# Row sums on the evicting engine, paired copies, freed buffers and a written order: induced attention with a folded leaky FFN on one core

## The chip, the cores and the metric

The kernel runs on one core of a Trainium2 chip. The engines are TensorE (PE; its weight loads are shown apart as PEld), VectorE (DVE), ScalarE (ACT), GpSimd (POOL) and SyncE (SP), whose queue issues nearly all DMAs. The metric is the device time of an execution in microseconds, from the start of the program to its end, lower is better. The profile's span runs from the first to the last instruction of the profiled execution.

## The reference

```python
def mab(q, kv):
    s = scale * (q @ kv.transpose(0, 2, 1))
    s = s - s.max(-1, keepdims=True)
    a = np.exp(s)
    a /= a.sum(-1, keepdims=True) + 1e-09
    return a @ kv
h = mab(I, x)                    # I: inducing (32 x 128), the same for all 4 batches
y = mab(x, h).astype(np.float32) # x: 4 x 12480 x 128
...
h = y.reshape(49920, 128) @ w_in           # w_in: 128 x 2048
return np.maximum(0.01 * h, h) @ w_out     # w_out: 2048 x 128
```

The 32 inducing rows attend to all rows of a batch, which gives 32 rows `h`; every row of x then attends to those 32 rows, and its result passes a leaky feed-forward layer. Inputs x and inducing are float32; the two weights are float64 in memory.

## The kernel before

Each row that enters the feed-forward layer is a weighted mean of the 32 rows `h` of its batch. Where every hidden column has one clear sign over those rows, the leaky layer is linear in them, so `fixed_sign_path` folds w_in, the slopes and w_out into one 32 x 128 matrix for each batch (with a column of ones behind it, 129 wide), and the output is the second attention's weights times that matrix, divided by their sum. A flag says at the end whether all signs were clear; if not, a branch runs `any_sign_path` over everything. With these inputs the branch skips it.

A batch of 12480 rows is cut into six groups of 2048 rows (g = 0 to 5) and a small one of 192 (g = 6). The work is a set of named operations, each with a batch and a group (or step) number, here with their lines:

- First pass, for each group: `LD` loads x (L1797); `T` transposes four blocks on TensorE (L1848) and `C` copies each to SBUF, on ScalarE or VectorE (L1860); `S1` multiplies with the inducing rows (L1868); `E` copies the scores and takes their maximum (L1887). For steps of two or three groups `RD`, `X`, `NM`, `AL` make the running maximum, `W` the exponentials (L1933), `Y` a 32 x 32 transpose (L1942), `V` the sum of rows (L1964), `ZT` the sums of weights and `GA` the running h.
- Middle, for each batch: `ZP`, `RZ`, `HS`, `HP`, `HC` normalise h and copy it transposed (`hT`, L2000); `H`, `HT`, `SH`, `AH`, `G`, `FO`, `FC`, `SP`, `SC` make the hidden row (L2005), the signs, the slopes (`G` on POOL, L2030), the folded matrix and its copy (`folded`, L2052).
- Second pass, for each group: `S2` the scores against h (L1868), `LO` and `LE` their lowest value, `U` the exponentials into `uT` (L2081). `O` is the product with the folded matrix (L2099), four for a big group: halves h = 0, 1 and parts t = 0, 1, each two PSUM banks. `D` evicts it. On VectorE it adds 1e-9 to the four row sums in PSUM, takes the reciprocals and scales into `osb` (L2121 to 2123). On ScalarE it copies everything, sums included, to `stage` (L2117); then POOL adds 1e-9 (`DS`, L2135), VectorE takes the reciprocal (`DI`, L2140) and POOL scales (`DM`, L2145). `ST` stores the group (L2156).
- The weights come in eight pieces: `LW` loads 0.5 MB (L1802, L1804) into a buffer of `osb`, and `CA`, `CB`, `CO`, `CT`, `CP` turn float64 words into float32: a shift on POOL or ScalarE (L1812), a mask (L1816) and a join (L1822) on VectorE, a tail on ScalarE (L1828) and a sum on POOL (L1837).

The order comes from a planner (`Plan.ordered`): a list scheduler with estimated lengths, a rank and a lean for each operation, which also picks the engine of `C`, `D` and `CA`. All engines run their own instructions in that order; waits are semaphores. The buffers are counted in `BUFS` (xr 6, e 4, ay 4, uT 3, osb 3, stage 3), the PSUM banks of `O` in `banks_of` (two pairs, a third for the last batch).

## Time and profile before

| | us |
|---|---|
| median of 3 runs (lowest to highest) | 213.36 (212.34 to 214.01) |
| profiled execution | 212.81 |
| its span, first to last instruction | 211.0 |
| TensorE busy, share of the span | 183.1, 87% |
| VectorE | 155.9, 74% |
| ScalarE | 119.3, 57% |
| POOL | 109.0, 52% |
| mean granted TensorE clock | 0.949 |
| HBM read, written | 29.77 MB, 25.56 MB |

Busy time is the union of an engine's instructions. [...]

### The profile page before, as it was taken

To read this page: it belongs to the slowest core of one execution; us is meant where nothing else is said; L and a number is where in the kernel's file an instruction comes from. 1 tells how busy PE (TensorE), PEld (TensorE's weight loads), DVE (VectorE), ACT (ScalarE), POOL (GpSimd) and SP (SyncE) were. 2 spreads that over 40 slices of the span, in tenths; PEclk is the share of its full clock that TensorE was granted. 3 is DMA by queue.
4 is the path that set the end of the run, shared out by engine and by line. 5 is a ranking of instruction groups with operands and counts; after the bars stand their busy time and mean duration, and the time that the engine had idled before them with its cause. 6 is when DMAs were issued, how large, how long until landed. Compare 5 with 4: busy or idle time off the path is not lost.

```text
span 211.0 us, 6947 instructions
## 1 busy us (share of the span) xinstructions
PE 183.1 (87%) x2791; PEld 121.5 (58%) x2791; DVE 155.9 (74%) x519; ACT 119.3 (57%) x252; POOL 109.0 (52%) x162
## 2 busy tenths in 40 slices
...
GB/s 208 418 420 392 270 393 354 366 398 18 188 213 130 380 353 143 218 408 245 241 405 269 281 381 363 393 57 221 161 238 168 76 163 202 221 202 381 297 261 95
DMA packets 18794, 55.87 MB, mean 265 GB/s; under 512 B 1056, under 2 KB 2240, under 8 KB 15808
## 3 DMA queue, kind: packets, MB, share of 16 engines
...
q14 instruction: 18, 0.15, 0.2%
...
HBM read 29.77 MB, written 25.56 MB: 262 GB/s over the span
## 4 chain that ended last, share of the span: by engine, by line
PE 65%; DVE 12%; ACT 6%; DMA 5%; POOL 4%; issue 2%; SPq 0%; ACTq 0%; DVEq 0%; POOLq 0%
PE s_ps L1868 18%; PE xT_ps L1848 17%; PE po L2099 15%; PE h_ps L1964 8%; DMA raw<-in_moe_w_out_dram 5%; ACT xT L1860 3%; POOL osb L2145 3%; DVE osb L2123 2%; PE busy_ps L1767 2%; PE m_ps L2038 2%; ACT stage L2117 2%; DVE cv_a L1822 2%; PE H_ps L2005 1%; DVE ay L1942 1%; POOL cv_a L1812 1%
## 5 line engine op out<-in xcount | busy, mean ns | idle before, releaser
L2145 POOL TENSOR_TENSOR osb<-stage,inv 128x512 f32<-128x512 f32 (+1 forms) x67 | 67.0, 1010 | 20.1 <-DVE inv L2140 12.9
L2117 ACT COPY stage<-po 128x516 f32<-128x516 f32 (+1 forms) x67 | 37.0, 576 | 35.3 <-PE po L2099 33.5
L1848 PE MATMUL xT_ps<-ident,xr 128*128 128x128 f32 x384 | 52.0, 280 | 1.7 <-ACT xT L1860 0.8
L2099 PE MATMUL po<-folded,uT 32*128 32x129 f32 (+1 forms) x792 | 47.9, 309 | 4.2 <-ACT stage L2117 1.6
L1848 PEld LDWEIGHTS xT_ps<-ident,xr 128*128 128x128 f32 x384 | 41.3, 141 | 17.1 <-issue 3.9
L1860 ACT COPY xT<-xT_ps 128x512 f32<-128x512 f32 x74 | 40.2, 591 | 18.1 <-PE xT_ps L1848 15.9
L2099 PEld LDWEIGHTS po<-folded,uT 32*128 32x128 f32 (+1 forms) x792 | 37.3, 194 | 21.0 <-issue 9.4
L2135 POOL TENSOR_SCALAR inv<-stage 128x4 f32<-128x4 f32 (+1 forms) x67 | 14.9, 222 | 44.4 <-ACT stage L2117 41.3
L1868 PE MATMUL s_ps<-xT,indT 128*32 128x512 f32 x192 | 26.3, 617 | 1.4 <-ACT xT L1860 1.4
L1868 PE MATMUL s_ps<-xT,hT 128*32 128x512 f32 x192 | 24.8, 599 | 2.1 <-ACT uT L2081 2.0
L1964 PE MATMUL h_ps<-xr,ay 128*32 128x128 f32 x768 | 24.0, 274 | 2.5 <-DVE zg L1931 1.3
L2123 DVE TENSOR_TENSOR osb<-po,inv 128x512 f32<-128x512 f32 (+2 forms) x37 | 24.1, 651 | 1.3
L1887 DVE TENSOR_SCALAR_CACHE_REDUCE e<-s_ps 128x512 f32<-128x512 f32 (+1 forms) x28 | 17.1, 615 | 10.2 <-PE s_ps L1868 8.4
L1964 PEld LDWEIGHTS h_ps<-xr,ay 128*32 128x32 f32 x768 | 20.6, 110 | 6.3 <-issue 1.7
L2081 ACT ACTIVATE uT<-s_ps,least 128x512 f32<-128x512 f32 (+1 forms) x28 | 17.9, 640 | 10.2 <-DVE least L2071 9.9
L1812 POOL TENSOR_SCALAR cv_a<-raw 128x512 f32<-128x512 f32 x7 | 11.5, 1653 | 19.5 <-DMA raw<-in_moe_w_in_dram 16.1
L1933 ACT ACTIVATE e<-e,nm 128x512 f32<-128x512 f32 (+1 forms) x28 | 18.6, 669 | 2.7 <-DVE zg L1931 2.4
L1860 DVE COPY xT<-xT_ps 128x512 f32<-128x512 f32 x22 | 14.7, 679 | 6.5 <-ACT xT L1860 3.6
L1942 DVE STREAM_TRANSPOSE ay<-e 128x512 f32<-128x512 f32 (+1 forms) x28 | 17.3, 630 | 0.8 <-ACT e L1933 0.5
L2062 DVE TENSOR_REDUCE low<-s_ps 128x1 f32<-128x512 f32 (+1 forms) x28 | 17.0, 608 | 1.0 <-PE s_ps L1868 0.9
L2140 DVE RECIPROCAL inv<-inv 128x4 f32<-128x4 f32 (+1 forms) x67 | 10.6, 165 | 4.3 <-POOL inv L2135 3.4
L2121 DVE TENSOR_SCALAR inv<-po 128x4 f32<-128x4 f32 (+2 forms) x37 | 5.6, 151 | 5.7 <-PE po L2099 5.5
...
## 6 DMA issues: line engine op xcount, KB each, us to landing
out_dram<-osb SPq DMA_DIRECT2D x24, 1024.0 KB, 5.8
xr<-in_x_dram SPq DMA_DIRECT2D x23, 1024.0 KB, 7.8
raw<-in_moe_w_in_dram SPq DMA_DIRECT2D x4, 512.0 KB, 14.2
raw<-in_moe_w_out_dram SPq DMA_DIRECT2D x4, 512.0 KB, 8.5
xr<-in_x_dram SPq DMA_DIRECT2D x2, 512.0 KB, 4.5
...
```

Of the source, the lines that this page charges most:

```text
L1848: nc.tensor.transpose(pt[:, k * rows : (k + 1) * rows], xr[b, g][:rows, 4 * q + k, :], ident[:rows, :rows])
L1860: copying(engine)(xT[b, g][:, 4 * q : 4 * q + n, :].rearrange("p k t -> p (k t)"), V.pop(("T", b, g, q))[:, : n * rows],)
L1868: nc.tensor.matmul(ps[32 * j : 32 * j + 32, :w].rearrange("p (k r) -> p k r", r=32), lhsT, xT[b, g][:, :, 32 * j : 32 * j + 32], start=Tru ...
L1887: nc.vector.tensor_scalar(out=e[:rows], in0=V.pop(("S", b, g))[:rows, :w], scalar1=1.0, scalar2=None, op0=ALU.mult, op1=ALU.max, accum_out ...
L1933: nc.scalar.activation(e[:rows, :w], e[:rows, :w], AF.Exp, bias=nms[b, p][:rows], scale=SCALE, accum_out=zg[:rows])
L1942: nc.vector.transpose(t[:rows].rearrange("p k m -> p (k m)"), e[:rows, :w])
L1964: nc.tensor.matmul(hp[32 * (k % 4) : 32 * (k % 4) + 32, :], t[:rows, k, :], rows_in[:rows, k, :], start=(i == 0 and k < 4), stop=(last[k % ...
L2081: nc.scalar.activation(dst, src, AF.Exp, bias=least[:rows, b, g : g + 1])
L2099: nc.tensor.matmul(po[:m, j % 2, (P + 1) * i : (P + 1) * (i + 1)], uT[b, g][part, columns], folded[b % 2][part, :], start=True, stop=True, ...
L2117: nc.scalar.copy(raw[:m, :nj, : (P + 1) * n], src)
L2123: nc.vector.tensor_tensor(out=dst, in0=src[:, :, :, :P], in1=inv.unsqueeze(3).broadcast_to([m, nj, n, C]), op=ALU.mult)
L2145: nc.gpsimd.tensor_tensor(out=dst, in0=raw[:, :, :, :P], in1=inv.unsqueeze(3).broadcast_to([m, nj, n, C]), op=ALU.mult)
```

## The change

- The row sums of an `O` part are read from PSUM by the engine that evicts the part (`SA`: ScalarE or VectorE, +1e-9 into a small tile `inv` shared by both parts of a half). One reciprocal on VectorE (`RC`) serves both parts. `D` on ScalarE copies the 512 values alone; `D` on VectorE scales from PSUM after `RC`; POOL's `DM` needs `D` and `RC`. `DS` and `DI` are gone.
- The two copies `C` of a transposition pair that shares a PSUM tile run on one engine, both after the second transpose.
- The weight shift `CA` runs on ScalarE alone; `G` may run on VectorE, but the order keeps it on POOL.
- In the last batch `uT` is taken from the buffers of `e` and `ay` in turn, and `osb` of odd groups from those of `xr`; the last two big groups are stored in two halves.
- The order is written out; a letter behind a name picks the engine (a ScalarE, v VectorE, p POOL). `Plan.ordered` reads it and asserts that dependencies and buffers allow it. The planner, its ranks and leans are gone.
- Each engine gets a branch hint for the final branch, behind a marked instruction of the last batch, and the flag is read outside the hand-ordered block.

```diff
-    RANKS = {
...
+    ORDER = """
...
+        O0.4.0.0 D0.4.0.0a SA0.4.0.0a O0.4.0.1 SA0.4.0.1a D0.4.0.1a X1.2 NM1.2 AL1.2 W1.4 RC0.4.0 DM0.4.0.0
...
-    def cv_shift(i, engine):
+    def cv_shift(i):
...
-        multiply = nc.scalar.mul if engine == "ACT" else nc.gpsimd.tensor_scalar_mul
-        multiply(a.bitcast(F32), raws[i][:, :, 1].bitcast(F32), 2.0**-112)
+        nc.scalar.mul(a.bitcast(F32), raws[i][:, :, 1].bitcast(F32), 2.0**-112)
...
+    def weights_in(b, g):
+        return "uTr" if g == RG else "uT" if b < B - 1 else ("e", "ay")[g % 2]
+
+    def results_in(b, g):
+        return "xr" if b == B - 1 and g % 2 and g != RG else "osb"
...
+    def part_sums(b, g, h, t, engine):
+        n, m, nj, _ = results(b, g, h, t)
+        dst = V["inv", b, g, h][:m, 2 * t : 2 * t + nj, :n]
+        src = V["po", b, g, h, t][:m, :nj, P : (P + 1) * n : P + 1]
+        if engine == "ACT":
+            nc.scalar.activation(dst, src, AF.Copy, bias=1e-9)
+        else:
+            nc.vector.tensor_scalar_add(dst, src, 1e-9)
+
+    def part_inverse(b, g, h):
+        n, m, nj, _ = results(b, g, h, 1)
+        inv = V["inv", b, g, h][:m, : 2 + nj, :n]
+        nc.vector.reciprocal(inv, inv)
...
         if engine == "ACT":
-            V["raw", b, g, h, t] = raw = sb.tile([P, 2, 2 * P + 2], F32, tag="stage", name="stage", bufs=BUFS["stage"])
-            nc.scalar.copy(raw[:m, :nj, : (P + 1) * n], src)
-            return
...
-        inv = sb.tile([P, 2, 2], F32, tag="inv", name="inv", bufs=4)[:m, :nj, :n]
-        nc.vector.tensor_scalar_add(inv, src[:, :, :, P], 1e-9)
-        nc.vector.reciprocal(inv, inv)
...
+            V["raw", b, g, h, t] = raw = sb.tile([P, 2, 2, P], F32, tag="stage", name="stage", bufs=BUFS["stage"])
+            nc.scalar.copy(raw[:m, :nj, :n], src)
+        else:
+            nc.vector.tensor_tensor(out=dst, in0=src, in1=inverse_of(b, g, h, t)[4], op=ALU.mult)
...
-    def stage_sums(b, g, h, t):
...
-        nc.gpsimd.tensor_scalar_add(inv[:m, :nj, :n], raw[:, :, :, P], 1e-9)
-
-    def stage_inverse(b, g, h, t):
...
-    def store(b, g):
+        n, m, nj, dst, inv = inverse_of(b, g, h, t)
+        raw = V.pop(("raw", b, g, h, t))[:m, :nj, :n]
+        V["latest", "Pool"] = nc.gpsimd.tensor_tensor(out=dst, in0=raw, in1=inv, op=ALU.mult)
+
+    def store(b, g, j0, j1):
...
+                after=[("T", b, g, q | 1 if bank[0] != "tp" else q)], rank=at,
+                like=("C", b, g, q - 1) if q % 2 and bank[0] != "tp" else None,
...
+        for engine, mark in marks.items():
+            with tc.issue_after(mark):
+                tc.mark_branch_hint_location("general", hint="LikelyTaken", engines=[engine])
+        undecided = nc.values_load(flag[:1, :1], min_val=0, max_val=1)
+        with tc.If(undecided != 0, label="general"):
             any_sign_path(tc, x, inducing, w_in, w_out, out)
```

The table of the order, in instructions. SP's queue at the start of the program, before (`xr` is a group of x, `xrr` the small one, `raw` a piece of the weights):

```order
L1797 DMA xr<-in_x_dram 128x1024 x2
L1797 DMA xr<-in_x_dram 128x2048 x4
L1802 DMA raw<-in_moe_w_in_dram 128x1024 x3
L1797 DMA xr<-in_x_dram 128x2048
L1802 DMA raw<-in_moe_w_in_dram 128x1024
L1797 DMA xrr<-in_x_dram 96x256
L1797 DMA xr<-in_x_dram 128x2048 x2
L1804 DMA raw<-in_moe_w_out_dram 128x1024 x3
L1797 DMA xr<-in_x_dram 128x2048 x2
L1804 DMA raw<-in_moe_w_out_dram 128x1024
```

SP's queue at the same place now:

```order
L1652 DMA xr<-in_x_dram 128x1024 x2
L1652 DMA xr<-in_x_dram 128x2048 x3
L1657 DMA raw<-in_moe_w_in_dram 128x1024
L1652 DMA xr<-in_x_dram 128x2048 x2
L1652 DMA xrr<-in_x_dram 96x256
L1657 DMA raw<-in_moe_w_in_dram 128x1024 x2
L1652 DMA xr<-in_x_dram 128x2048 x2
L1657 DMA raw<-in_moe_w_in_dram 128x1024
L1659 DMA raw<-in_moe_w_out_dram 128x1024
L1652 DMA xr<-in_x_dram 128x2048
L1659 DMA raw<-in_moe_w_out_dram 128x1024 x3
```

Batch 0's last groups stand behind one piece of the weights instead of three and four, and the last three pieces behind one more group of batch 1. VectorE's queue up to batch 0's normalised h (`hc`), before (`cv_b` and `cv_a` are mask and join of a piece of the weights, `zn` the sum of weights, `e` the scores of a group of batch 1):

```order
L1816 TENSOR_SCALAR cv_b<-raw 128x512
L1822 SCALAR_TENSOR_TENSOR cv_a<-cv_a,cv_b 128x512
L1947 TENSOR_REDUCE z<-zg 128x1
L1950 TENSOR_SCALAR zn<-zn,al,z 128x1
L1887 TENSOR_SCALAR e,rm<-s_ps 128x512
L1987 TENSOR_SCALAR rz<-z_ps 128x1
L1988 RECIPROCAL rz<-rz 128x1
L1976 SCALAR_TENSOR_TENSOR hacc<-hacc,al,h_ps 128x128
L1992 TENSOR_SCALAR hc<-hacc,rz 128x128
```

VectorE's queue at the same place now:

```order
L1799 TENSOR_REDUCE z<-zg 128x1
L1802 TENSOR_SCALAR zn<-zn,al,z 128x1
L1670 TENSOR_SCALAR cv_b<-raw 128x512
L1676 SCALAR_TENSOR_TENSOR cv_a<-cv_a,cv_b 128x512
L1828 SCALAR_TENSOR_TENSOR hacc<-hacc,al,h_ps 128x128
L1743 TENSOR_SCALAR e,rm<-s_ps 128x512
L1828 SCALAR_TENSOR_TENSOR hacc<-hacc,al,h_ps 128x128
L1839 TENSOR_SCALAR rz<-z_ps 128x1
L1840 RECIPROCAL rz<-rz 128x1
L1670 TENSOR_SCALAR cv_b<-raw 128x512
L1844 TENSOR_SCALAR hc<-hacc,rz 128x128
```

The mask and join of piece 6 no longer stand ahead of the last sum; those of piece 4 stand behind it, and the mask of piece 5 between the reciprocal and `hc`. VectorE's queue at the first evictions of batch 3, before (`low` and `least` are the lowest scores, `osb` the output; the numbered `inv` belong to parts that ScalarE has copied):

```order
L2121 TENSOR_SCALAR inv<-po 128x4
L2122 RECIPROCAL inv<-inv 128x4
L2123 TENSOR_TENSOR osb<-po,inv 128x2x256
L2140 RECIPROCAL inv_3167<-inv_3167 128x4
L2070 STREAM_TRANSPOSE lows<-low 128x32
L2071 TENSOR_REDUCE least<-lows 128x1
L2062 TENSOR_REDUCE low<-s_ps 128x1
L2140 RECIPROCAL inv_3178<-inv_3178 128x4
```

VectorE's queue at the same place now:

```order
L1980 TENSOR_SCALAR inv<-po 128x4
L1985 RECIPROCAL inv<-inv 128x8
L1999 TENSOR_TENSOR osb<-po,inv 128x2x256
L1922 STREAM_TRANSPOSE lows<-low 128x32
L1923 TENSOR_REDUCE least<-lows 128x1
L1980 TENSOR_SCALAR inv<-po 128x4
L1985 RECIPROCAL inv<-inv 128x8
L1999 TENSOR_TENSOR osb<-po,inv 128x2x256
```

One reciprocal of eight stands where two of four stood, and it is ahead of the scaling of its own half.

## Rows read from the trace of the kernel before

**Rows 1.** Stretch, length, busy PE PEld DVE ACT POOL (instructions), clock, DMA share, GB/s.

```profile
5.30:24.40 19.10, 16.37 (x185) 11.07 (x184) 9.34 (x22) 11.34 (x23) 4.97 (x4) 1.00 0.96 387
24.40:45.60 21.20, 16.15 (x253) 10.96 (x254) 17.45 (x45) 12.60 (x29) 15.61 (x11) 0.93 0.98 368
45.60:165.00 119.40, 116.78 (x1889) 78.24 (x1893) 96.72 (x322) 77.71 (x169) 59.62 (x96) 1.00 0.67 249
...
178.30:203.00 24.70, 18.17 (x238) 12.90 (x230) 19.25 (x80) 10.15 (x19) 17.61 (x29) 0.79 0.68 261
203.00:211.00 8.00, 0.00 (x0) 0.00 (x0) 0.00 (x0) 0.00 (x0) 0.00 (x0) 0.50 0.45 157
```

**Rows 2.** Timeline, weight joins and hT of batch 0: start, us, engine, [idle before].

```profile
20.41 0.69 DVE L1822 SCALAR_TENSOR_TENSOR cv_a<-cv_a,cv_b 128x512 int32<-128x512 int32 x1
...
40.80 1.56 DVE L1822 SCALAR_TENSOR_TENSOR cv_a<-cv_a,cv_b 128x512 int32<-128x512 int32 x1
...
42.89 0.29 PE L1725 MATMUL z_ps<-zn,e 128*32 128x1 f32 x8 [2.29 <-DVE zn L1950]
...
45.62 0.21 ACT L2000 COPY hT<-hT_ps 128x64 f32<-128x64 f32 x1 [3.75 <-PE hT_ps L1725]
```

**Rows 3.** The page's groups: count, busy us, mean ns, idle us before.

```profile
L2135 POOL TENSOR_SCALAR inv<-stage 128x4 f32<-128x4 f32 (+1 forms) x67 | 14.9, 222 | 44.4 <-ACT stage L2117 41.3
L1812 POOL TENSOR_SCALAR cv_a<-raw 128x512 f32<-128x512 f32 x7 | 11.5, 1653 | 19.5 <-DMA raw<-in_moe_w_in_dram 16.1
L2140 DVE RECIPROCAL inv<-inv 128x4 f32<-128x4 f32 (+1 forms) x67 | 10.6, 165 | 4.3 <-POOL inv L2135 3.4
```

**Rows 4.** Groups with shapes kept apart, the same columns.

```profile
L2145 POOL TENSOR_TENSOR osb<-stage,inv 128x512 f32<-128x512 f32 x63 | 64.8, 1040 | 17.6 <-DVE inv L2140 12.9 <-DVE inv L2121 2.6 <-DVE rd L1896 0.7
L2117 ACT COPY stage<-po 128x516 f32<-128x516 f32 x63 | 35.7, 591 | 34.2 <-PE po L2099 32.5 <-POOL inv L2135 0.7
L2123 DVE TENSOR_TENSOR osb<-po,inv 128x512 f32<-128x512 f32 x33 | 22.8, 691 | 1.1
L1822 DVE SCALAR_TENSOR_TENSOR cv_a<-cv_a,cv_b 128x512 int32<-128x512 int32 x8 | 7.7, 963 | 1.5 <-POOL cv_a L1812 1.1
L2121 DVE TENSOR_SCALAR inv<-po 128x4 f32<-128x4 f32 x33 | 5.0, 153 | 5.7 <-PE po L2099 5.5
L1922 ACT ACTIVATE al<-nm 128x1 f32<-128x1 f32 x8 | 2.4, 296 | 5.4 <-DVE lower L1915 5.4
L2000 ACT COPY hT<-hT_ps 128x64 f32<-128x64 f32 x4 | 0.9, 220 | 3.7 <-PE hT_ps L1725 3.7
L1812 ACT ACTIVATE cv_a<-raw 128x512 f32<-128x512 f32 x1 | 0.7, 677 | 0.0
```

**Rows 5.** Chain that ended last: start, us, what; transposes in runs of eight and four.

```profile
59.20 1.02 PE xT_ps L1848 x8
...
62.91 0.59 PE xT_ps L1848 x4
```

**Rows 6.** Timeline of the last batch: start, us, engine, [idle before].

```profile
178.06 0.27 ACT L2052 COPY folded<-M_ps 128x128 f32<-128x128 f32 x1
...
183.14 1.06 PE L1868 MATMUL s_ps<-xT,hT 128*32 128x512 f32 x8 [1.33 <-ACT uT L2081]
...
192.81 3.23 PE L2099 MATMUL po<-folded,uT 32*128 32x129 f32 x32
...
202.19 1.25 SPq L2156 DMA_DIRECT2D out_dram<-osb  x2
```

**Rows 7.** DMA issues: count, KB each, median us from issue to landing.

```profile
out_dram<-osb SPq DMA_DIRECT2D x24, 1024.0 KB, 5.8
...
xr<-in_x_dram SPq DMA_DIRECT2D x2, 512.0 KB, 4.5
```

**Rows 8.** Instructions of the final branch: min/median/max ns, first and last start.

```profile
L2358 SPq EVENT_SEMAPHORE  x8: 17/17/17, 208.3 to 209.6; - x8
...
L2358 SPq COMPARE_BRANCH  x1: 45/45/45, 204.4 to 204.4; - x1
```

More of the change, by code (lines that the diff above doesn't have):

```diff
@@ new lines, in read @@
+    def read(self):
+        kinds = sorted({name[0] for name in self.ops}, key=len, reverse=True)
+        picks = {"a": "ACT", "v": "DVE", "p": "POOL"}
+        for word in self.ORDER.split():
+            kind = next(k for k in kinds if re.fullmatch(k + r"(\d+(\.\d+)*)?[avp]?", word))
+            at = word[len(kind) :].rstrip("avp")
+            name = (kind, *(int(i) for i in at.split(".") if i))
+            yield name, picks[word[-1]] if word[-1] in picks else next(iter(self.ops[name][0]))
@@ new lines, in ordered, with is_done @@
+    def ordered(self):
+        by, taken, order = {}, {}, []
+        def is_done(name):
+            only = self.ops[name][6]
+            while only is not None and only[0] in by and by[only[0]] != only[1]:
+                name, only = only[0], self.ops[only[0]][6]
+            return name in by
+        for name, engine in self.read():
+            lengths, emit, after, _, _, takes, _, extra, _, _, needs, like = self.ops[name]
+            assert engine in lengths and all(is_done(a) for a in after)
+            assert by.get(like, engine) == engine
+            assert engine not in needs or needs[engine] in by
+            for buffer in takes + extra.get(engine, []):
+                earlier = taken.setdefault(buffer[0], [])
+                n = len(earlier) - self.rooms[buffer[0]]
+                assert n < 0 or all(is_done(u) for u in self.users[earlier[n]])
+                earlier.append(buffer)
+            by[name] = engine
+            order.append((name, lambda emit=emit, engine=engine: emit(engine)))
+        assert all(is_done(name) for name in self.ops)
+        return order
@@ L2300, in second_pass @@
                 po, f = (banks_of(*part), *part), 1.0 if big else 0.4
-                first = [("osb", *key)] if h + t == 0 else []
+                first = [(otag, "O", *key)] if h + t == 0 else []
                 before = before_part
                 before_part = [("O", *part)]
-                add(("O", *part), {"PE": 0.446 * f}, lambda _, a=part: output(*a), mode="R",
-                    after=[("U", *key), ("SC", b)] + before, rank=at + 0.2, takes=[po] + first, uses=[po, (utag, *key), ("folded", b)], joins=("O", *key, h, 0) if t else None)
@@ L2311, in second_pass @@
-                add(("DI", *part), {"DVE": 0.18}, lambda _, a=part: stage_inverse(*a), after=[("DS", *part)], **staged_op)
-                add(("DM", *part), {"POOL": 1.05 * f}, lambda _, a=part: stage_scaled(*a), after=[("DI", *part)], **staged_op)
-                last += [("D", *part), ("DM", *part)]
-        add(("ST", *key), {"DMA": 2.55 if big else 1.2}, lambda _: store(b, g), rank=at - BEFORE,
-            after=last, uses=[("osb", *key)])
+                add(("O", *part), {"PE": 0.5 * f}, lambda _, a=part: output(*a), mode="R",
+                    after=[("U", *key), ("SC", b)] + before, rank=at + 0.2, takes=[po] + first + ([] if t else [("inv", *key, h)]), uses=[po, (utag, "U", *key), ("folded", b)], joins=("O", *key, h, 0) if t else None)
@@ new lines, in second_pass @@
+                add(("DM", *part), {"POOL": 1.02 if big else 0.55}, lambda _, a=part: stage_scaled(*a),
+                    after=[("D", *part), ("RC", *key, h)], only=(("D", *part), "ACT"), rank=at - 1,
+                    uses=[(otag, "O", *key), ("stage", *part), ("inv", *key, h)])
+                last += [("D", *part), ("DM", *part)]
+            add(("RC", *key, h), {"DVE": 0.17}, lambda _, h=h: part_inverse(*key, h), rank=at - 1,
+                after=[("SA", *key, h, t) for t in range(2)], uses=[("inv", *key, h)])
```

389 lines of the change are left out of this document (150 added, 239 removed), and 90 rows, old and new, of tables (LEANS, RANKS).

## Prediction

> **What bounds the kernel now.** I read the table of stretches first, then the timeline around the two places where it shows TensorE idle, then the groups for prices, and last the end of the program.
>
> The table [rows 1] splits the span at batch 0's small copy of h (45.6 us), at the end of the first passes (165), at the copy of batch 3's folded matrix (178.3) and at the last output work (203). From 45.6 to 165 TensorE is busy 116.78 of 119.40 us: that stage is bound by TensorE, and work taken off VectorE, ScalarE or GpSimd there is worth nothing. Outside it there is room. Up to 45.6 us TensorE is idle 2.73 + 5.05 us, and the granted clock of the second stretch is 0.93, so some 1.5 us more (0.07 of 21.2) are lost to the lower of its two levels: about 9 us. From 178.3 to 203 no engine is full (PE 18.17 of 24.70 at clock 0.79, DVE 19.25, POOL 17.61): the bound is the round trip from one engine to the next. The last 8.0 us hold no work.
>
> The timeline [rows 2] names the early gap. VectorE's weight joins (L1822) stand ahead of batch 0's last sum; one is 0.69 us at 20.41, another 1.56 us at 40.80. TensorE waits 2.29 us behind `zn`, and hT is copied only at 45.62. This wait, and not the DMA share of 0.98, ends last, although the joins themselves need weights that have landed.
>
> **The change, part by part.**
>
> *Row sums and GpSimd.* Removed: 67 additions on POOL at 0.222 us (14.9) and 7 weight shifts at 1.653 (11.5) [rows 3]. In the middle that is off the path and worth 0; its cover is TensorE's 116.78 us. The shifts count in the start: they go to ScalarE at 0.677 us each [rows 4] (+4.7 us on an engine with 12.60 of 21.20 busy). New on ScalarE are 63 sums of four elements. No row shows that instruction; the nearest are the 64-column copy at 0.220 and the one-column exponential at 0.296, and below 0.2 I see no reason to go. I take 0.22 (it too is a plain function read from PSUM): +14 us over the span on an engine that is busy 77.71 of 119.40 in the middle: 0 on the path. On VectorE 104 reciprocals of 0.165 become 52 (-8.6), 37 sums of 0.153 become 41 (+0.6), and 37 scaled evictions of 0.69 become 41 (+2.8): some -5 us, off the path in the middle.
>
> *What this adds as a wait.* A VectorE eviction now waits for the sums of both halves, one of them ScalarE's, then one reciprocal, so a PSUM bank is held about 0.22 + 0.165 + 0.69 plus queueing, some 1.3 to 1.9 us, against 0.59 (copy) or about 1.0 (sum, reciprocal, scaling) now. Queued behind it on VectorE are the peaks and copies that TensorE waits for. What covers it is the new order: of the 38 places before batch 3 where one pair of output products follows another, 28 have at least 1.7 us of other TensorE work between them (22 in the old order), and 4 have under 1.1 us (16 in the old). I price the wait at 0, up to +5.
>
> *New order, TensorE's turns.* Counting the changes between transposes, column products and row products in the two orders gives 126 before and 142 now. Eight transposes in a run take 1.02 us, four take 0.59 [rows 5]: a second run costs 0.16 us. With 16 changes, eight runs' worth is +1.3 us; 0.16 for each change, the upper end, is 2.6. I take +1.3.
>
> *New order, the start.* On SP, group 0.5 and the small one now come with one weight load ahead instead of three and four; group 0.4 gets that one ahead where it had none. VectorE's queue holds one weight mask (`CB5`, a wait for load 5) between 1/Z and the normalising step; ScalarE's holds the shift and tail of load 6 ahead of the copy of hT. So hT waits for load 6: nine groups of 1.05 MB, the small one and seven loads of 0.524 MB are 13.2 MB, at 368 to 387 GB/s [rows 1] 34 to 36 us, plus about 1.5 for two ScalarE steps and 1.5 of latency: 37 to 39. TensorE's own work up to there is 16.37 + 16.15 - 1.5, plus three more transposes at 0.51: 32.5 us from 5.3, so 37.8 with no idle. Keeping the idle of the first stretch (2.7) and 1.5 of the second gives 42 instead of 45.6, with 1.5 us more work behind it: about 5 less, of which I take 4, since the pair rule makes the first copies wait for a second transpose. Ends: 0 (the wait only moves to ScalarE's queue) and 7 (all idle but 2 us goes).
>
> The eight joins have a mean of 963 ns against 0.69 undisturbed [rows 2, 4], 2.2 us in all, where POOL's shifts ran beside them. [...]
>
> *Last batch in freed buffers.* Its second weights go to the buffers of `e` and `ay`, odd results to those of `xr`. In the trace the second scores wait 1.33 us for `uT` at 183.14 [rows 6]; that wait is part of the tail below, and nothing is given for the buffers apart from it.
>
> *The tail.* From 178.3 the VectorE work falls from 19.25 by 13 reciprocals (2.2) and two small evictions that go to ScalarE (about 1.0, 1.4 at the price of large ones): about 16. POOL's falls by 13 sums (2.9), and two of its 13 scalings become small ones (about 1.0): 13.7. At the old ratio of length to VectorE work, 24.70/19.25, 16 gives 20.5 us, -4.2. Following the new order from the copy of the folded matrix (copy 0.5, sum 0.2, reciprocal 0.17, scaling 0.69 or 1.03), the first store is ready after about 4 us, the next ones every 2.5 to 2.8, the last after 17 to 18: -7. I take -5. Ends: -1.5 (four output products took 3.23 us at 192.81 [rows 6], after the clock had fallen to the lower of its levels; with that from the start TensorE becomes the bound) and the stores: 6.39 MB at 384 GB/s (261 at a share of 0.68) are 16.6 us behind the first, so with 4 us ahead of them and some 3 us after the last one's issue no less than 24 of the 32.7 us up to the end of the span remain: -8.7, what follows included.
>
> *The end.* The last store is issued by 203.4; 1 MB takes 5.8 us to land, 0.5 MB take 4.5 [rows 7]. Halved, it lands 1.3 us sooner. That counts only if SP's branch comes as soon: SP compares at 204.4 and runs on at 208.3 [rows 8], 3.9 us of fetching that now stand beside the landing. The hint is there to hide it; -1.2 with it.
>
> Sum: 212.81 (the profiled execution, 211.0 of span and 1.8 around it) - 4 + 1.3 - 5 - 1.2 = 203.9. The median of three is 0.55 above that execution; I forecast **204.2 us**, -4.3%.
>
> **The rivals.**
>
> *A: the start gives nothing.* ScalarE's queue (shift, tail, copy) makes hT wait where VectorE's joins did. For it: VectorE's work in the second stretch is 17.45 of 21.2 and hardly falls. Against it: fewer bytes stand ahead of batch 0, and no POOL shift stands in the chain. 204.2 + 4 = 208.2.
>
> *B: the tail gives only its floor.* The clock falls at once in the last batch. In the trace it fell only at 192.8, after TensorE had waited, and the new tail keeps it busier. 204.2 + 3.5 = 207.7. With A as well: 211.7, no change.
>
> *C: the hint does nothing,* and the end costs what it did: 204.2 + 1.2 = 205.4. [...]
>
> *D: slower.* The bank hold reaches TensorE. Its place is the output pair in the middle stage, where each of 38 pairs would lose 0.4 us, when VectorE's reciprocal waits for a ScalarE sum queued behind an exponential: +15, so 219. It decides when the hold is longer than the work set between two pairs: above 1.7 us for 10 of the 38. For it: ScalarE's queue is longer by 14 us. Against it: TensorE is idle 2.6 us in the whole middle now, with pairs set closer.
>
> **How the numbers follow.** Forecast 0.47; C 0.15; A or B alone 0.18; both of them, which is no change, 0.08; more than the forecast (start 7, tail 7 to 8: 198 to 199) 0.05; D 0.07. The range holds the forecast, C, A and B, 0.80: it reaches from 198.5, where both parts come near their upper ends, to 210.5, above A and B with 2 us for the turns at their upper end; it leaves out D and no change. One per cent, about what a measurement here can tell, is 211.2 to 215.5. Faster: 0.85; same: 0.08; slower: 0.07.
>
> **What would show it.** In the new profile: hT copied at 41 to 42 us, and no lower clock before it; TensorE busy over 97% up to the first passes' end, with waits of `po` on `inv` under 3 us in all; the folded matrix of batch 3 copied at 174 to 176; first store of batch 3 about 4 us behind it and the last output work 18 to 20 us behind it; sums on ScalarE near 0.22 us; and SP running on within 1 us of its compare. It would be wrong with TensorE idle in the middle on VectorE's scaling (D), with hT still at 45 (A), or with the clock down before 180 (B).

## The result, and the profile after

The changed kernel takes 200.58 us, the median of 4 executions (199.92 to 201.78), against 213.31 before (212.34 to 214.01): a ratio of 0.9413 with an interval of 0.9352 to 0.9473. Measured a second time beside the last experiments it took 200.13 us (0.9390, 0.9353 to 0.9428). The forecast was 204.2 us. Two of the four executions of one run below, e4, took over 1.5% longer than its fastest and are left out of its ratio, though not of its median, and no length is read from its profile, which is of one of them. The profiled execution took 200.23 us, and its span is 198.4 us, 12.6 less than before.

The table of stretches of the changed kernel, cut at the small copy of h and at the end of the copy of the first and of the last folded matrix (columns as in [rows 1]):

```profile
5.30:43.28 37.98, 33.13 (x469) 23.66 (x469) 28.68 (x74) 25.58 (x54) 6.35 (x5) 1.00 0.95 358
43.28:53.00 9.72, 8.44 (x128) 4.52 (x124) 8.89 (x20) 7.07 (x16) 5.34 (x4) 1.00 0.59 243
53.00:170.87 117.87, 115.42 (x1980) 75.23 (x1972) 94.84 (x316) 78.54 (x212) 50.74 (x50) 1.00 0.73 264
170.87:186.50 15.63, 13.78 (x220) 9.68 (x214) 13.89 (x48) 9.96 (x29) 10.87 (x12) 1.00 0.85 320
186.50:191.40 4.90, 2.57 (x22) 1.08 (x20) 3.71 (x16) 1.68 (x7) 4.03 (x5) 0.50 1.05 395
191.40:198.40 7.00, 0.00 (x0) 0.00 (x0) 0.00 (x0) 0.00 (x0) 0.00 (x0) 0.50 0.30 102
```

The same cuts of the kernel before:

```profile
5.30:45.60 40.30, 32.52 (x438) 22.03 (x438) 26.79 (x66) 23.94 (x51) 20.59 (x14) 0.96 0.97 377
45.60:57.11 11.51, 11.27 (x184) 7.43 (x184) 8.48 (x22) 6.65 (x15) 2.46 (x3) 0.98 0.33 118
57.11:178.33 121.22, 117.35 (x1941) 77.86 (x1936) 99.98 (x348) 77.29 (x167) 67.37 (x109) 1.00 0.68 252
178.33:203.00 24.67, 18.14 (x238) 12.90 (x230) 19.22 (x80) 10.12 (x18) 17.58 (x29) 0.79 0.68 261
```

Read side by side, the first folded matrix is there 4.1 us sooner (57.11, now 53.00), the middle from the first to the last folded matrix is 3.35 us shorter (121.22, now 117.87), the last batch's output 4.1 us (from 178.33 to the last output work at 202.97, now from 170.87 to 191.38), and what follows it 1.0 us (8.0, now 7.05). That is 12.6. The granted clock, which the profile gives as a share of full speed and which in both traces is 1.00 or 0.50 at any moment, is 1.00 here from 5.3 us on, where its mean was 0.93 in one stretch of [rows 1]; it falls to 0.50 only at 186.5, in the last batch.

The middle deserves a second look, because TensorE was busy for nearly all of it before as well. The same stretch, with the instructions on `po` (the output products) alone, before:

```profile
57.11:178.33 121.22, 33.05 (x594) 25.10 (x594) 19.49 (x48) 29.53 (x54) 1.00 0.68 252
```

and after:

```profile
53.00:170.87 117.87, 30.15 (x594) 22.50 (x594) 23.30 (x60) 30.25 (x96) 1.00 0.73 264
```

The same 594 products are busy 2.9 us less. The timeline of TensorE shows how. Three neighbouring pairs before, with eight transposes or fewer between them:

```profile
67.03 0.74 PE L2099 MATMUL po<-folded,uT 32*128 32x129 f32 x16
67.70 1.09 PE L1848 MATMUL xT_ps<-ident,xr 128*128 128x128 f32 x8
68.29 0.69 DVE L2123 TENSOR_TENSOR osb<-po,inv 128x512 f32<-128x512 f32 x1
...
68.73 1.12 PE L2099 MATMUL po<-folded,uT 32*128 32x129 f32 x16
...
70.53 1.31 PE L2099 MATMUL po<-folded,uT 32*128 32x129 f32 x16
```

and after, with transposes and scores between them:

```profile
65.03 0.74 PE L1959 MATMUL po<-folded,uT 32*128 32x129 f32 x16
65.70 1.09 PE L1702 MATMUL xT_ps<-ident,xr 128*128 128x128 f32 x8
66.72 1.06 PE L1722 MATMUL s_ps<-xT,hT 128*32 128x512 f32 x8
67.72 0.74 PE L1959 MATMUL po<-folded,uT 32*128 32x129 f32 x16
```

Sixteen products take 0.74 us when their two PSUM banks are free. Behind a pair that began 1.7 or 1.8 us earlier they take 1.12 and 1.31. VectorE's scaling out of the first of these pairs ends at 68.98, when the second has begun: TensorE waits for the eviction of a bank in the middle of the run, and the records of the run cover most of that wait, so that it counts as busy. Counted from the start of each run to the start of TensorE's next one, which gives idle time behind a run to the run, the products of the middle took 32.7 us before and 28.2 now, and of the runs of 16 or more, 15 of 35 took over 0.75 us before and 7 of 36 do now. That is where the middle's 3.35 us come from: the products give back 4.5, and the rest of TensorE's row takes 1.2 more. TensorE's shown idle time (3.87, now 2.45) is part of it.

The groups that answer to [rows 3, 4], shapes kept apart:

```profile
L1978 ACT ACTIVATE inv<-po 128x4 f32<-128x4 f32 x59 | 9.8, 178 | 20.9 <-PE po L1959 20.2
L1985 DVE RECIPROCAL inv<-inv 128x8 f32<-128x8 f32 x48 | 9.6, 199 | 4.5 <-ACT inv L1978 1.3 <-ACT e L1785 0.3
L1676 DVE SCALAR_TENSOR_TENSOR cv_a<-cv_a,cv_b 128x512 int32<-128x512 int32 x8 | 5.4, 680 | 0.2
L1670 DVE TENSOR_SCALAR cv_b<-raw 128x512 int32<-128x512 int32 x8 | 6.2, 776 | 2.0 <-DMA raw<-in_moe_w_in_dram 2.0
```

A sum on ScalarE takes 178 ns. VectorE's reciprocal waited for such a sum 1.3 us in the whole span: the wait that rival D named is there, and small. The joins are down from a mean of 963 ns to 680 (2.3 us less in all); the masks are up, from 614 to 776 (1.3 us more).

The final branch, which answers to [rows 8]:

```profile
L2230 SPq EVENT_SEMAPHORE  x8: 17/17/17, 196.5 to 197.1; - x8
...
L2230 PEldq COMPARE_BRANCH  x1: 469/469/469, 192.2 to 192.2; - x1
L2230 ACTq EVENT_SEMAPHORE  x1: 17/17/17, 192.6 to 192.6; - x1
L2230 PEldq EVENT_SEMAPHORE  x1: 51/51/51, 192.7 to 192.7; - x1
L2230 SPq COMPARE_BRANCH  x1: 70/70/70, 193.4 to 193.4; - x1
L2230 DVEq EVENT_SEMAPHORE  x1: 21/21/21, 195.0 to 195.0; - x1
L2230 POOLq EVENT_SEMAPHORE  x1: 17/17/17, 196.1 to 196.1; - x1
```

SP still runs on only 3.1 us behind its compare, 3.9 before; its eight instructions then take 0.6 us where they took 1.3, with a gap in which, as I read it, SP waited for the last store. ScalarE and TensorE's weight loads, hinted as well, run on after 0.5.

### The profile page after: what moved, and what is told of

Its sections match the earlier page's. It is cut to its first block, busy times and chain, and to the rows that moved or that the text cites. A ratio compares the mean times of both kernels' runs of the same rounds, so it can differ in the third digit from the quotient of the medians.

```text
span 198.4 us, 6958 instructions
## 1 busy us (share of the span) xinstructions
PE 177.2 (89%) x2791; PEld 115.5 (58%) x2791; DVE 151.5 (76%) x476; ACT 124.1 (63%) x317; POOL 78.4 (39%) x84
## 4 chain that ended last, share of the span: by engine, by line
PE 61%; DMA 16%; DVE 9%; issue 2%; POOL 2%; SPq 2%; ACT 2%; POOLq 0%; DVEq 0%
PE s_ps L1722 17%; PE xT_ps L1702 17%; PE po L1959 14%; DMA xr<-in_x_dram 13%; PE h_ps L1816 9%; DMA raw<-in_moe_w_in_dram 4%; DVE osb L1999 3%; PE m_ps L1890 2%; POOL osb L2004 2%; PE H_ps L1857 1%; SPq L1652 1%; DVE inv L1985 1%; ACT xT L1714 1%; DVE cv_b L1670 1%; DVE inv L1980 1%
## 5 line engine op out<-in xcount | busy, mean ns | idle before, releaser
L2004 POOL TENSOR_TENSOR osb<-stage,inv 128x512 f32<-128x512 f32 (+2 forms) x63 | 62.6, 1006 | 71.4 <-ACT stage L1997 32.9
L1714 ACT COPY xT<-xT_ps 128x512 f32<-128x512 f32 x70 | 38.5, 590 | 22.2 <-PE xT_ps L1702 22.0
L1959 PEld LDWEIGHTS po<-folded,uT 32*128 32x128 f32 (+1 forms) x792 | 32.5, 184 | 21.8 <-issue 5.0
L1959 PE MATMUL po<-folded,uT 32*128 32x129 f32 (+1 forms) x792 | 43.3, 296 | 2.0 <-DVE inv L1980 0.8
L1997 ACT COPY stage<-po 128x512 f32<-128x512 f32 (+2 forms) x63 | 35.0, 570 | 5.2 <-PE po L1959 5.2
L1999 DVE TENSOR_TENSOR osb<-po,inv 128x512 f32<-128x512 f32 (+2 forms) x41 | 26.5, 655 | 1.5
L1978 ACT ACTIVATE inv<-po 128x4 f32<-128x4 f32 (+2 forms) x63 | 10.4, 177 | 22.2 <-PE po L1959 21.6
L1714 DVE COPY xT<-xT_ps 128x512 f32<-128x512 f32 x26 | 17.2, 684 | 6.3 <-PE xT_ps L1702 6.3
L1816 PEld LDWEIGHTS h_ps<-xr,ay 128*32 128x32 f32 x768 | 20.5, 110 | 1.3 <-issue 0.6
L1939 ACT ACTIVATE uT<-s_ps,least 128x512 f32<-128x512 f32 (+1 forms) x28 | 17.7, 642 | 1.4 <-DVE least L1923 1.0
L1691 POOL TENSOR_TENSOR w_in_sb<-cv_a,cv_t 128x512 int32<-128x512 int32 x4 | 5.1, 1281 | 30.7 <-ACT cv_t L1682 25.0
L1985 DVE RECIPROCAL inv<-inv 128x8 f32<-128x8 f32 (+1 forms) x52 | 10.2, 197 | 4.5 <-ACT inv L1978 1.3
```

The costliest lines, as they stand in the source:

```text
L1714: copying(engine)(xT[b, g][:, 4 * q : 4 * q + n, :].rearrange("p k t -> p (k t)"), V.pop(("T", b, g, q))[:, : n * rows],)
L1816: nc.tensor.matmul(hp[32 * (k % 4) : 32 * (k % 4) + 32, :], t[:rows, k, :], rows_in[:rows, k, :], start=(i == 0 and k < 4), stop=(last[k % ...
L1939: V["latest", "Activation"] = nc.scalar.activation(dst, src, AF.Exp, bias=least[:rows, b, g : g + 1])
L1959: V["latest", "PE"] = nc.tensor.matmul(po[:m, j % 2, (P + 1) * i : (P + 1) * (i + 1)], uT[b, g][part, columns], folded[b % 2][part, :], st ...
L1997: nc.scalar.copy(raw[:m, :nj, :n], src)
L1999: nc.vector.tensor_tensor(out=dst, in0=src, in1=inverse_of(b, g, h, t)[4], op=ALU.mult)
```

## The experiments

Twelve runs, each beside runs of the kernel before on the same chip (213.3 to 213.5 us). The lengths are worked out from each profiled execution: "start" to the end of the first copy of a folded matrix, "middle" to the end of the fourth, "output" to the end of the last output work, "end" to the end of the span. The column `po` is the busy time of the middle's 594 output products, read as above.

| run | median us | ratio to before (interval) | start | middle | po | output | end |
|---|---|---|---|---|---|---|---|
| before | 213.36 | | 57.1 | 121.2 | 33.05 | 24.6 | 8.0 |
| changed | 200.58 | 0.9413 (0.9352 to 0.9473) | 53.0 | 117.9 | 30.15 | 20.5 | 7.1 |
| changed again (e12) | 200.13 | 0.9390 (0.9353 to 0.9428) | 52.4 | 118.2 | 30.16 | 20.9 | 6.6 |
| e1 old order, new sums | 218.00 | 1.0231 (1.0156 to 1.0307) | 57.0 | 125.4 | 34.47 | 24.3 | 8.8 |
| e2 new order, old sums | 220.80 | 1.0361 (1.0319 to 1.0402) | 52.8 | 131.5 | 31.54 | 27.1 | 7.1 |
| e9 the same, more room | 218.56 | 1.0222 (1.0175 to 1.0268) | 54.0 | 129.1 | 31.18 | 27.2 | 7.3 |
| e3 eight close pairs | 219.28 | 1.0294 (1.0234 to 1.0355) | 52.6 | 136.3 | 35.30 | 20.5 | 7.1 |
| e4 sums twice | 205.07 | 0.9538 (0.9450 to 0.9625) | | | | | |
| e5 no hint | 202.06 | 0.9465 (0.9412 to 0.9518) | 52.7 | 118.1 | | 21.0 | 7.1 |
| e6 late hint | 201.16 | 0.9431 (0.9379 to 0.9483) | 52.9 | 118.2 | | 21.1 | 6.5 |
| e7 whole stores | 201.99 | 0.9470 (0.9416 to 0.9524) | 52.2 | 118.2 | | 21.1 | 7.4 |
| e8 own buffers | 200.88 | 0.9422 (0.9374 to 0.9471) | 53.9 | 117.9 | | 21.1 | 6.7 |
| e10 hT ahead | 202.83 | 0.9506 (0.9454 to 0.9557) | 53.8 | 117.8 | | 20.6 | 7.1 |
| e11 hT ahead, late hint, two places respaced | 203.17 | 0.9520 (0.9489 to 0.9550) | 55.0 | 118.7 | | 21.1 | 6.5 |

### Order and sums apart: e1, e2, e9

e1 takes the changed kernel and gives it the order that the planner of before makes, with the new sums set in where the old eviction stood:

```diff
-        O0.1.0.0 D0.1.0.0a O0.1.0.1 SA0.1.0.0a SA0.1.0.1a RC0.1.0 DM0.1.0.0 D0.1.0.1a DM0.1.0.1 LO0.4
+        O0.1.0.0 E1.4 O0.1.0.1 T1.5.1 SA0.1.0.0a D0.1.0.0a SA0.1.0.1v RC0.1.0 D0.1.0.1v ST0.0 T1.5.2 C1.5.1a
...
-    HALVED = [(B - 1, g) for g in range(NG - 2, NG)]
+    HALVED = []
...
-        return "uTr" if g == RG else "uT" if b < B - 1 else ("e", "ay")[g % 2]
+        return "uTr" if g == RG else "uT"
```

> The old written order (also the old buffers, whole stores, no hint, the old engines of the weight shifts) with the new row sums and the one reciprocal of eight. Before took 213.3 us, the changed kernel 200.6. Theory 'spacing': inside an output pair TensorE waits for its PSUM banks when the pair before it lies less than some 2 us ahead; 16 of the 38 pairs of the old order do. So from the first to the last copy of the folded matrix the 594 output products still take 32 to 34 us (32.7 before, 28.2 in the changed kernel), and only the last batch and the joins gain: 209 to 213 us. Theory 'shorter hold': the new sums free the banks sooner, so these products take 28 to 29.5 us in the old order too: 205 to 209 us. Theory 'longer hold' (my rival D): they take 36 us or more: 215 us and up.

It took 218.0 us, 2.3% more than before. The "shorter hold" falls: the products of the middle take 34.47 us by the view, more than the 33.05 of before; counted from start to start 35.3, against 32.7 then. That lies between "spacing" (32 to 34) and "longer hold" (36 or more); the time lies in the range of the second. So in the old places the new sums hold a bank longer, not shorter. VectorE's waits, before and in e1, name the reason:

```profile
DVE inv L2140 <- POOL inv L2135: 3.4, 7, 1.2
```

```profile
DVE inv L1984 <- ACT inv L1977: 11.0, 19, 1.3
```

The columns are total us, times and longest. VectorE's reciprocal waited 3.4 us for GpSimd's sums before; it waits 11.0 us for ScalarE's sums in e1, and 1.3 us in the changed kernel. This is the mechanism of rival D, at a third of its price: 4.6 us where D had 15. And the output of the last batch takes 24.3 us as against 24.6, although VectorE's work there is down from 19.2 to 17.7 us and GpSimd's from 17.6 to 14.0:

```profile
182.40:206.66 24.26, 19.52 (x236) 13.95 (x228) 17.74 (x65) 10.90 (x31) 13.98 (x14) 0.72 0.72 263
```

e2 goes the other way, with the new order and everything else of the change, but the old sums. e9 is e2 with one VectorE instruction more between a copy on ScalarE and the reciprocal for it:

```diff
-        O0.1.0.0 D0.1.0.0a O0.1.0.1 SA0.1.0.0a SA0.1.0.1a RC0.1.0 DM0.1.0.0 D0.1.0.1a DM0.1.0.1 LO0.4
+        O0.1.0.0 D0.1.0.0a DS0.1.0.0 O0.1.0.1 D0.1.0.1a DS0.1.0.1 LO0.4 DI0.1.0.0 DM0.1.0.0 DI0.1.0.1 DM0.1.0.1
...
-            nc.scalar.copy(raw[:m, :nj, :n], src)
+            nc.scalar.copy(raw[:m, :nj, : (P + 1) * n], src)
```

> The new order with the old row sums: ScalarE copies 516 columns, GpSimd sums, VectorE takes a reciprocal of four behind its next instruction, GpSimd scales; VectorE's own evictions do sum, reciprocal of four and scaling. Theory 'spacing': the 594 output products between the first and the last copy of the folded matrix take 28 to 29.5 us, as in the changed kernel; the last batch loses 1 to 4 us, since GpSimd has 13 sums more and VectorE 13 reciprocals more there: 201.5 to 205 us. Theory 'shorter hold': the products go back to 31 us or more: 204 to 208 us.

> The new order with the old row sums once more, but with each reciprocal for a ScalarE-copied half (and the scaling behind it) two VectorE instructions behind that copy's place in the order instead of one. In the run with one, VectorE waited 17.6 us for GpSimd's sums and the time was 220.8 us. Theory 'VectorE's queue': the loss of that run is VectorE standing before a reciprocal that GpSimd has not fed, so one more instruction of room brings VectorE's wait under 9 us and the time to 208 to 214 us. Theory 'the new order asks for the new sums': room on VectorE does not help, since it is the round trip over GpSimd that holds ScalarE's three staging buffers and so the banks: 217 to 222 us.

e2 took 220.8 us and e9 218.56: all theories had e2 too low, and e9 lies in the range of "the new order asks for the new sums". VectorE's waits in e2 and in e9:

```profile
DVE inv L1995 <- POOL inv L1990: 17.6, 19, 2.3
```

```profile
DVE inv L1995 <- POOL inv L1990: 16.2, 15, 3.4
```

One instruction of room took 1.4 us off that wait, which stayed far above the 9 us of "VectorE's queue", so e9 does not rule that theory out, and its trace speaks for it. At TensorE's two longest waits in the middle of e9 (1.74 and 1.57 us) what TensorE needed came behind such a reciprocal on VectorE. The second of them:

```profile
177.36 0.48 DVE L1995 RECIPROCAL inv<-inv 128x4 f32<-128x4 f32 x2 [3.41 <-POOL inv L1990]
...
178.97 0.69 ACT L1935 ACTIVATE uT<-s_ps,least 128x512 f32<-128x512 f32 x1 [3.34 <-DVE least L1919]
...
179.72 1.08 PE L1718 MATMUL s_ps<-xT,hT 128*32 128x512 f32 x4 [1.57 <-ACT uT L1935]
```

At the first, a product waits until 164.34 us for VectorE's own eviction, which stands behind a reciprocal that waited 1.76 us. The wait for `stage`, by which the other theory had the time lost, is 0.7 us in that middle, once. Part of the loss is clock: the mean granted clock of the middle is 0.96 in e2 and 0.97 in e9, where before, e1 and the changed kernel have 1.00.

```profile
52.75:184.21 131.46, 121.83 (x1976) 79.01 (x1972) 99.29 (x357) 75.91 (x164) 62.02 (x99) 0.96 0.67 244
```

By this line that is at most some 5 us (0.04 of 131.5, an estimate) of the 13.6 by which e2's middle is longer than the changed kernel's. I placed the new sums of e1 and the reciprocals of e2 and e9 by a rule, and a better placing may exist. The four corners together: old order with old sums 213.4, old order with new sums 218.0, new order with old sums 218.6, both new 200.6. Each half alone costs about 5 us, and the two together gain 13. One part these runs do give apart: the start. In every run with the new start the first folded matrix is there at 52.2 to 55.0 us, with the old sums too (52.8, 54.0), and in e1, with the old one, at 57.0.

### Pairs close together: e3

At eight places of the new order the second pair of a group goes right behind the evictions of the first, and the transposes and scores that stood between come after it.

```diff
-        D0.1.0.1a DM0.1.0.1 LO0.4 T1.5.0 T1.5.1 C1.5.0a S11.4 O0.1.1.0 O0.1.1.1 LE0.4
+        D0.1.0.1a O0.1.1.0 O0.1.1.1 DM0.1.0.1 LO0.4 T1.5.0 T1.5.1 C1.5.0a S11.4 LE0.4
```

> The changed kernel, with the second output pair of 8 groups (0.1, 0.2, 0.3, 1.1, 1.2, 2.0, 2.1, 2.2) written right behind the evictions of the first, so that the transposes and scores that stood between come behind it. Theory 'spacing': each of the 8 waits inside itself for its banks, 1.0 to 1.6 us (a run of 32 products took 2.95 us before, 1.6 more than twice 0.67), so the products between the first and the last copy of the folded matrix take 36 to 41 us instead of 28.2 and the time is 206 to 213 us. Theory 'shorter hold': the banks are free again within some 1 us, at most 0.3 us for each: 200.6 to 203 us.

It took 219.28 us, 18.7 more than the changed kernel, above the range of "spacing" and far from its rival. A place in TensorE's timeline, and the two longest waits for a bank in the whole span:

```profile
65.91 0.74 PE L1957 MATMUL po<-folded,uT 32*128 32x129 f32 x16
67.37 1.44 PE L1957 MATMUL po<-folded,uT 32*128 32x129 f32 x16 [0.72 <-ACT stage L1995]
```

```profile
PE po L1957 <- DVE osb L1997: 5.5, 6, 1.7
PE po L1957 <- ACT stage L1995: 3.0, 5, 0.7
```

The second pair is held up 0.72 us as shown idle time and 0.70 more inside its 1.44. Over the eight, from start to start, the products take 42.2 us instead of 28.2, or 1.75 each, a little above the 1.0 to 1.6 expected. The other 4.4 of the middle's 18.4 us are transposes, scores and values that came out longer; the mean granted clock of the middle is 0.96, where the changed kernel has 1.00. The middle, and one of the places where the clock fell:

```profile
52.60:188.89 136.29, 125.60 (x1980) 81.95 (x1972) 94.74 (x316) 78.89 (x212) 50.79 (x50) 0.96 0.63 228
106.00:109.00 3.00, 2.17 (x44) 1.61 (x40) 1.20 (x5) 1.93 (x6) 1.04 (x1) 0.97 0.92 309
109.00:112.00 3.00, 3.00 (x15) 1.39 (x8) 1.21 (x4) 0.24 (x1) 0.00 (x0) 0.50 1.02 382
```

It fell to its lower level three times, for some 3.4 us each (from about 109, 119 and 163.5 us), behind three of the eight close pairs: TensorE had been busy 2.17 us from 106 to 109, 1.77 from 115 to 118 and 1.32 from 161 to 164. Behind the other five close pairs it stayed at 1.00.

### A longer hold: e4

```diff
             nc.scalar.activation(dst, src, AF.Copy, bias=1e-9)
+            nc.scalar.activation(dst, src, AF.Copy, bias=1e-9)
```

> The changed kernel with each of ScalarE's 63 row sums taken twice, the second writing the same values: 0.18 us more hold of a bank and 11 us more of ScalarE. Theory 'spacing': the pairs lie 2 us apart or more but for a few, so the added hold is covered: 200.6 to 202 us. Rival D in small: the hold or ScalarE's queue is near its bound, and a third or more of the 11 us comes out: 204 us and up.

The ratio is 0.9538, 1.3% above the changed kernel's 0.9413, or some 2.7 us (0 to 6 by the two intervals); the median says 4.5. "Covered" allowed 1.4, "rival D in small" wanted 3.4 or more, and the run does not tell them apart for sure. By its middle values a quarter to 40% of the 11 us come out, so the order covers the hold as it is and seems to have little to spare.

### The end: e5, e6, e7

e5 leaves out the hints. e6 takes the marks of VectorE, GpSimd and SP later. e7 stores the last two large groups whole.

```diff
-        for engine, mark in marks.items():
-            with tc.issue_after(mark):
-                tc.mark_branch_hint_location("general", hint="LikelyTaken", engines=[engine])
```

```diff
+        if name == ("ST", B - 1, NG - 1, 0):
+            for e in (e for e in marks if str(e).split(".")[-1] in ("DVE", "Pool", "SP")):
+                marks[e] = V["latest", str(e).split(".")[-1]].ins
```

```diff
-        RC3.6.0 ST3.4.0 ST3.4.1 ST3.5.0 DM3.5.1.1 ST3.5.1
+        RC3.6.0 ST3.4 DM3.5.1.1 ST3.5
```

> The changed kernel without the five branch hints. In its trace SP runs on 3.1 us after its compare (3.9 before), VectorE 2.8, GpSimd 4.0, but ScalarE and TensorE's loads 0.5. Theory 'SP's fetch ends the program, hinted or not': ScalarE and TensorE fall back to some 2 to 4 us, SP stays at 3 to 4: 200.6 us, within 0.7. Theory of my forecast, that the hint is worth the 1.2 us: 201.6 to 202.2.

> The changed kernel with the hints of VectorE, GpSimd and SP some 5 us ahead of their branches instead of 12 to 28 (those of ScalarE and TensorE stay). Theory 'too early': what the hint fetched is gone when the branch comes, so a later one is kept; SP runs on within 1 us of its compare, and the end is set by the landing of the last store, near 195 instead of 196.5: 198.8 to 199.6 us. Theory 'these engines drop the hint': they still wait 2.8 to 4 us: 200.6 us, within 0.5.

> The changed kernel with the last two large stores whole. Term of my forecast: the halved store lands 1.3 us sooner, so whole ones cost up to that: 201.5 to 202. Theory 'SP's fetch ends the program': the last large store would be issued at about 190 and land some 5.6 later, near 195.5, still ahead of SP's first instruction behind the branch at 196.5, so nothing is lost: 200.6 us, within 0.5.

Without hints, the branch instructions:

```profile
L2227 SPq EVENT_SEMAPHORE  x8: 17/17/17, 197.0 to 197.5; - x8
...
L2227 PEldq COMPARE_BRANCH  x1: 3479/3479/3479, 192.5 to 192.5; - x1
...
L2227 SPq COMPARE_BRANCH  x1: 45/45/45, 193.8 to 193.8; - x1
```

and with the late ones:

```profile
L2235 SPq EVENT_SEMAPHORE  x8: 17/17/17, 196.7 to 197.2; - x8
...
L2235 SPq COMPARE_BRANCH  x1: 70/70/70, 194.1 to 194.1; - x1
```

TensorE's weight loads run on after 3.6 us without a hint and 0.5 with one. ScalarE does the same (4.0 and 0.5) in all hinted runs but e4 and e8 (3.7 and 3.6). SP runs on after 3.2 without and 2.6 to 3.4 with a hint, 2.6 with the late one: on SP the hint changes next to nothing, early or late, and SP is the last. "Too early" falls. By the traces the end is 7.1 us in the changed kernel, 7.1 without hints, 6.5 with late ones and 7.4 with whole stores; by the times e6 is the changed kernel's, and e5 and e7 lie 0.6 to 0.9% above it with intervals that touch (0.9412 to 0.9518 and 0.9416 to 0.9524, against 0.9352 to 0.9473 and 0.9353 to 0.9428). Of e5's surplus some 0.4 us lies outside the span (2.1 to 3.3 us of its executions, against 1.8 to 1.9 in e6 and e7), where no view has a cause. The changed kernel measured again (e12) came at 200.13, but on another chip than e5 and e7, so it does not settle what their 202 are. Whether the hint and the halved stores bring a microsecond or nothing stays open.

### The last batch's buffers: e8

```diff
-        return "uTr" if g == RG else "uT" if b < B - 1 else ("e", "ay")[g % 2]
+        return "uTr" if g == RG else "uT"
...
-        return "xr" if b == B - 1 and g % 2 and g != RG else "osb"
+        return "osb"
```

> The changed kernel with the last batch in the buffers of the other batches (second weights in three of uT, results in three of osb). Theory 'the freed buffers carry part of the tail': the second scores wait for uT (1.3 us before) and the first results for stores of batch 2 to land: 202 to 204 us. Theory of my forecast, that they are worth nothing apart from the other parts: 200.6 to 201.4 us.

200.88 us, and an output of 21.1 us as against 20.5 and 20.9: the freed buffers are worth nothing that can be measured.

### A better version that was not: e10, e11, e12

In the changed kernel TensorE's product for hT ends at 42.1 us, and hT is copied at 43.28, behind a shift and a tail on ScalarE. e10 lets both go first.

```diff
-        GA0.2 LW5 CA5 ZP0 RZ0 CB5 HS0 CO5 LW6 LW7 CB6 T1.2.0 T1.2.1 T1.2.2 C1.2.0a T1.2.3
-        C1.2.1a C1.2.3a C1.2.2a S11.1 E1.1 RD1.0 CA6 CO6 CT6 CP6 HP0 HC0 S11.2
+        GA0.2 LW5 ZP0 RZ0 HS0 T1.2.0 T1.2.1 HP0 HC0 CA5 CB5 CO5 LW6 LW7 CB6 T1.2.2 C1.2.0a T1.2.3
+        C1.2.1a C1.2.3a C1.2.2a S11.1 E1.1 RD1.0 CA6 CO6 CT6 CP6 S11.2
```

> The changed kernel with batch 0's normalising step on VectorE ahead of the mask of weight piece 5, its TensorE product after two quads of transposes instead of four and one set of scores, and ScalarE's copy hT ahead of the shift and tail of piece 6. In the changed kernel hT is copied at 43.28 us, 1.1 us behind its product. Theory 'ScalarE's queue holds the copy' (rival A in small): hT at 41 to 42 us, the folded matrix of batch 0 1 us sooner, 199.4 to 200.4 us. Theory 'the weights bind': the folded matrix waits for the last piece of the weights all the same, and nothing comes out: 200.6 us, within 0.5.

hT came even sooner than expected, and nothing came of it:

```profile
39.97 0.21 ACT L1852 COPY hT<-hT_ps 128x64 f32<-128x64 f32 x1 [2.66 <-PE hT_ps L1580]
...
43.70 0.62 PE L1857 MATMUL H_ps<-w_in_sb,hT 128*32 128x512 f32 x4
```

The hidden row's product, which reads hT, still stands behind two sets of scores in TensorE's row and starts at 43.70, as it did (43.67); the folded matrix is 0.8 us later (a difference that runs with the same start have among themselves, 52.2 to 54.0), and the time 202.83 us, above both runs of the changed kernel; the profiled execution, 201.07 us, is nearer to theirs. Neither theory had this: not ScalarE's queue and not the weights, but TensorE's own row sets that point. e11 adds the late hints and moves work between pairs at two places of the middle.

```diff
-        RD3.1 T3.5.2 T3.5.3 C3.5.2a C3.5.3a O2.2.1.0
+        RD3.1 O2.2.1.0
...
-        D2.2.1.1v ST2.2 S22.5 LO2.5 LE2.5 AL3.1 W3.2 T3.6.0 C3.6.0a
+        D2.2.1.1v ST2.2 T3.5.2 T3.5.3 C3.5.2a C3.5.3a S22.5 LO2.5 LE2.5 AL3.1 W3.2
```

> The changed kernel with hT ahead and the late hints, and with two places of the middle respaced: in batch 0 transposes of group 2.1 and the first scores of group 2.0 between pairs that stood 1.7 us apart, in batch 2 two quads of transposes moved between two pairs that waited. Theory 'spacing': 0.7 us less of waits in pairs, so with hT ahead 198.5 to 200 us. Theory 'nothing is left there': the waits move to the next pair or the next stage: 200.6 us, within 0.5.

> The changed kernel as it is, in the same call as the kernels that should beat it, and to set beside the one without hints (202.1 us) and the one with whole stores (202.0). Every theory: 200.6 us, within 0.7; if it comes at 201.5 or more, the 1.4 us of the kernels without hints and with whole stores are the chip's, not theirs.

203.17 us: the middle is 118.7 us, no shorter, and the start is 2 us longer. The changed kernel on the same chip took 200.13. No version found here beats it.

## Why the prediction was right, and where it was not

The direction and the range were right, the forecast 3.6 us too long, nearly all of it in the middle. By its terms, against the profiled execution:

- **Start, -4 forecast, -4.1 measured.** The sum held; its steps less. hT was forecast at 41 to 42 us and came at 43.28, so the wait moved to ScalarE's queue in part, as rival A said. The other 1.8 us lie behind hT (11.5 us to the folded matrix, now 9.7): the product that reads hT started 2.1 us behind the copy before (47.68 against 45.62) and starts 0.4 behind it now. e10 shows that hT alone is no lever. No lower clock came before it, as forecast. The 1.5 us of latency in the prediction's sum for hT was an estimate that no row shows; in the trace of before the first bytes move 1.8 us into the span.
- **TensorE's turns, +1.3; the middle's waits, 0 with ends 0 and +5.** Here a step failed. The transposes of the middle take 1.0 us more, from start to start, and one wait of 1.5 us for an eviction by VectorE is in them, so the turns cost nothing that shows. And the middle came out 3.35 us shorter instead of 1.3 longer, and the last folded matrix at 170.9 instead of 174 to 176. The step is "I price the wait at 0, up to +5": it took the wider spacing of the pairs (28 with room instead of 22, 4 tight ones instead of 16) as a cover for a new cost alone. The tight pairs were already waiting, 15 of 35 runs of products, inside times that the table counts as busy. Since the middle was read as bound by TensorE at 116.78 of 119.40 us, no gain was allowed there, and the lower end of that bound was set at 0 without a row that excludes a gain. e3 shows the price of a tight pair, 1.75 us.
- **The tail, -5; measured -4.1.** The size was near, the reason not. The estimate by VectorE's work (19.25 down to 16, so 20.5 us) gave the right length by luck: e1 has half of VectorE's relief and nearly all of GpSimd's, and gains 0.4. It is the new order with the new sums that shortens it; the clock stays full for 15.6 us of the last batch's output, where it fell after 14.4 of 24.6 before. Rival B's early fall of the clock did not come. The first store of batch 3 is issued 4.6 us behind the folded matrix and the last output work is 20.5 behind it, against about 4 and 18 to 20.
- **The end, -1.2; measured -1.0.** The mechanism was wrong: SP was to run on within 1 us of its compare and takes 3.1. The 1.3 us of the halved store set a load of x (4.5) beside a whole store; in the new profile half a store lands 4.8 us behind its issue and the last whole ones 5.6, so 0.8 is what halving gives. Rival C was right on SP, but not for all engines: in the changed kernel two of five hinted engines, ScalarE and TensorE's weight loads, run on in 0.5 us, where they took 4.0 and 3.6 without hints (e5); the other three take 2.2 to 4.6 us in all hinted runs, against 3.2 to 4.6 without. That SP's 3.9 us are fetching is shown in part: in the trace of before seven instruction loads of 8 KB and one of 16 KB start between SP's compare and its next instruction (204.4 to 208.3), but no view says for which engine.
- **D, 219.** It did not come, but not because the hold is short. e1 shows D's mechanism: the new sums without the new order, with the reciprocal waiting for ScalarE's sum. That its 218.0 us lie beside D's 219 is chance, since D had the gains of start and end in it and e1 has neither. The forecast gave the new order as the cover for the wait, and e1 and e3 show that it is one.
- **Freed buffers, 0:** e8 agrees.
- **Joins:** the mean fell to 680 ns, so all of the 2.2 us went; in this profile no join starts beside a running addition of GpSimd. In the second profile of the changed kernel (e12) one does and takes 1.57 us. The prediction has the joins lose beside GpSimd's shifts; in the trace of before the two longest (1.58 us at 24.21, 1.56 at 40.80) lie beside its additions, and only the third (1.15 at 37.68) beside a shift.

What is not settled: how the 7.4 us of the middle and the output divide between order and sums has no answer, since neither half gains anything alone; and the paired copies and the shift on ScalarE, parts of the new start, were not taken apart.
